# A chunked linear-attention and GELU kernel: end decays from transposed rows, state products inside the attention runs, more turns on the DMA crossbar, another order of loads, and every queue's order written out

## The chip, the cores and the metric

One Trainium2 chip; the program runs on one of its cores. The time is device microseconds of one execution. Five engines with a queue each work in parallel and wait for one another through semaphores: TensorE (PE; PEld is its weight load), VectorE (DVE), ScalarE (ACT), GpSimd (POOL) and SyncE (SP). Transfers are issued from the queues of SyncE, ScalarE and GpSimd and run on 16 DMA engines that all share.

## The reference

`q`, `k`, `v` and `alpha` are 4 x 8 heads x 768 tokens x 48, float32. A gated recurrence runs over the tokens of each head, and its output feeds a two-layer network with a tanh GELU:

```python
for t in range(S):
    state = alpha[:, :, t, :, None] * state + np.einsum('bhd,bhe->bhde', k[:, :, t], v[:, :, t])
    y[:, :, t] = np.einsum('bhd,bhde->bhe', q[:, :, t], state)
x = np.ascontiguousarray(y.transpose(0, 2, 1, 3)).reshape(B * S, H * D)      # 3072 x 384
h = x @ w_in                                                                 # 3072 x 2048
g = 0.5 * h * (1.0 + np.tanh(c * (h + 0.044715 * h * h * h)))
return g @ w_out                                                             # 3072 x 384
```

## The kernel before

The 768 tokens are cut into six chunks of 128. A pair is one chunk of two batch rows, so there are twelve pairs, 0 to 11; pair m is chunk m // 2. Inside a chunk the recurrence becomes products. With `cum` the running sum of ln(alpha) in the chunk, b = exp(cum) and binv = exp(-cum), one has q' = q b and k' = k binv; the masked product of q' and k' (`at`, then `atm`) times v gives what the chunk adds by itself, and q' times the carried state gives the rest. At the chunk's end the state is (state + k'^T v) times the end decay, exp of the sum over the whole chunk.

Steps of a pair, by the names that the written order uses (a number behind the dot tells steps of one kind in one pair apart):

- `load`: alpha, q, k, v, issued by GpSimd (line 308), each 128 tokens by 16 rows of 48. The loads are numbered in the order of LOADS: 12 is v of pair 0, 13 and 15 to 17 are the quarters of w_in, 18, 19, 24 and 29 the quarters of w_out, 20 to 23 are a, q, k, v of the first row of pair 2, 25 to 28 those of its second row, 30 to 33 a, q, k, v of pair 3, 34 to 37 of pair 4, 38 to 41 of pair 5, 42 to 45 of pair 6, 46 to 49 of pair 7, and so on to 65.
- `ln` (ScalarE, 361), `cum` (TensorE, 378): the sums, a product with a triangle of ones. For pairs 2 to 9 eight more products with a column of ones (380) give the chunk's whole sums with the head dimension on the partitions; `bend` (ScalarE, 401) takes their exp, `end` (VectorE, 516) spreads them. Pairs 0 and 1 are packed in another way and have products of their own (346, 350).
- `b`, `binv` (ScalarE, 407); `qp`, `kp` (VectorE, 418).
- the turn of q' and k' to head dimension on partitions: `t` (TensorE, 428) with eviction `ev` (446) for pairs 0 to 6, a crossbar transpose `turn` issued by SyncE (466) for pairs 7 to 11.
- `attn` (489), four `mask` (VectorE, 496), `y`: per row, products of q' with the state (543) and of `atm` with v (546) into one bank; `x` copies it (553).
- the turn of x: `tx` (560) with `xe` (564) for pairs 0 to 5, a crossbar `turn` for each row (472) for pairs 6 to 11.
- `kv` (506) and `st` (528, 531): the new state.

The network for pair m: `l1m.0` to `l1m.7` (line 572: 6 products of 256 columns each, for two of the 16 blocks of 128 hidden units), each with a `gelu` (578); `l2m.0` to `l2m.7` (591: 4 products of 384 columns, a quarter of the hidden units for one batch row's 128 tokens). The rows of pairs 0 and 1 share one second layer, l20.0 to l20.15, where l20.4 n to l20.4 n + 3 use quarter n of w_out. `ot` copies a result (603), `store` writes it (616).

All order is static. `tasks()` lists every step with its inputs, a cost for each engine that may do it, and the buffers that it takes; `Scheduler.order()` lays them out. Steps in FIRST (A ScalarE, V VectorE, P TensorE, S SyncE, G GpSimd) go on their engine's queue in just that order; after FIRST the planner picks the rest itself by its costs. Each engine then runs its queue in order. The planner knows the landing of a load from its own sum of transfer times, except where LANDED names the load:

```python
            if t.name in self.landed:
                t.done = self.landed[t.name]
```

LANDED holds loads 0 to 33 (among them "load.24": 30100, "load.25": 31000, "load.28": 32900, "load.29": 34800, "load.30": 36700, in ns). The written order of before ends within pair 3. PSUM is cut into `ca` (one of two banks), `yk` (two banks, for t, y, tx, kv) and `ff` (four, for the network's sums and some of `at`). DECAYS ties the ScalarE steps that need its ln/exp table to places between blocks of gelu, since it holds one table at a time.

Of the kernel before, what the change touches and what calls it, by code (L numbers as in the profile page):

```python
# [16 lines left out]
    cum=530, cum_packed=1500, t8=450, t4=225, attn=340, kv=170, inter=170, intra=205, tx=168, l1_4=655, l1_2=340, l2=655,  # L17
    qk2=910, qk1=500, ev8=650, ev4=350, mask=640, st=1090, st0=545, end=110, attn2=590, vb=320, vb_act=480, ring=1300, ring_issue=670, out=2050, lead=600, receipt=1400, receipt_hw=1000, xc=520, xe=330, ot=540,
    ev8_act=960, ev4_act=520, xc_act=450, xe_act=450, ot_act=450,
    strip=1700, cast=1900, weight=2080, dma=2100, issue=1100, wissue=760, sp=100, store=2600, turn=1250, landed=2200, xbar_qk=1500, xbar_x=1000, late_x=2500, late_qk=1200, piece=330, late_k=1500, piece_issue=450, begin=620, cast_0=1300, share=1200, cast_1=1900, ln_packed=1040, cold=380, fill=216, zero=1100,  # L20
# [26 lines left out]
class Scheduler:  # L47
# [16 lines left out]
    def order(self):  # L64
# [107 lines left out]
class _Kernel:  # L172

    BLOCKS = ((0,), (1,), (2,), (3,), (4,), (5,), (6,), (7,), (8,), (9,), (10,), (11,))
    DECAYS = {-1: (0, 1), 1: (2, 3), 2: (4,), 3: (5,), 4: (6, 7), 5: (8,), 6: (9,), 7: (10,), 8: (11,)}

    SPLIT = (2,)
    EARLY = (0, 1)
    LOADS = ('gatea 0 1', 'v0', 'gatek 0 1', 'in 0', 'v1', 'in 1', 'in 2', 'in 3', 'out 0', 'out 1', '2a', 'out 2', '2b', 'out 3', '3', '4', '5', '6', '7', '8', '9', '10', '11')
# [7 lines left out]
        A:table.0 A:load.2 A:load.3 S:load.0 S:load.1 S:load.4 A:ln0.0 S:load.5 P:fill.7 P:cum0.0 A:ln0.1 G:gate.0 G:load.12 S:load.6 P:cum0.1 A:b0.0 S:load.7  # L187
        A:bend0.0 V:qp0.0 A:binv0.0 A:binv0.1 S:load.8 V:kp0.0 P:fill.2 P:t0.0 A:b0.1 V:ev0.0 P:fill.1 P:t0.1 S:load.9 A:ev0.1 V:qp0.1 S:load.10 A:bend0.1
        P:fill.3 P:attn0.0 V:kp0.1 G:gate.1 S:load.11 P:t0.2 G:load.13 V:mask0.0 A:ev0.2 P:t0.3 G:load.14 V:mask0.1 A:ev0.3 P:fill.1 P:t0.4 V:ev0.4 P:fill.1
        P:attn0.1 A:ln1.0 G:load.15 P:t0.5 V:mask0.3 P:cum1.0 A:ev0.5 G:load.16 V:vb0.0 A:ln1.1 V:end0.0 P:y0.0 V:mask0.2 G:load.17 P:kv0.0 A:binv1.0 P:cum1.1  # L190
        V:st0.0 A:x0.0 G:load.18 A:vb0.1 V:kp1.0 P:tx0.0 A:b1.0 P:y0.1 V:xe0.0 G:load.19 V:qp1.0 P:t1.1 A:x0.1 A:bend1.0 G:load.20 A:b1.1 P:fill.1 P:t1.0
        A:ev1.0 V:ev1.1 G:load.21 V:qp1.1 P:fill.1 P:kv0.1 V:st0.1 G:load.22 A:binv1.1 P:tx0.1 P:attn1.0 V:xe0.1 G:load.23 P:t1.2 V:kp1.1 P:l10.0 A:ev1.2
        G:load.24 V:mask1.0 P:t1.3 A:bend1.1 P:t1.4 V:mask1.1 G:load.25 A:ev1.3 P:l10.1 V:ev1.4 G:load.26 A:vb1.0 P:t1.5 P:attn1.1 G:load.27 V:ev1.5 P:y1.0
        G:load.28 P:l10.3 V:end1.0 V:vb1.1 V:mask1.2 G:load.29 A:gelu0.0 P:kv1.0 P:l10.2 V:mask1.3 A:x1.0 G:load.30 P:l10.5 A:gelu0.1 V:st1.0 A:gelu0.3 P:y1.1
        G:load.31 P:l10.4 A:gelu0.5 V:x1.1 P:tx1.0 A:gelu0.2 P:tx1.1 P:l10.6 G:load.32 V:xe1.1 A:gelu0.4 V:xe1.0 P:l10.7 A:gelu0.6 G:load.33 P:l11.0 A:gelu0.7
        P:l11.6 A:gelu1.0 P:l11.5 A:gelu1.6 P:l11.7 A:gelu1.5 P:l11.2 A:gelu1.7 P:l11.4 A:gelu1.2 P:l11.3 A:gelu1.4 P:l11.1 A:gelu1.3 P:kv1.1 P:l20.0
        A:gelu1.1 P:l20.4 P:l20.1 A:ln2.0 P:l20.2 P:cum2.0 P:l20.5 A:b2.0 A:binv2.0 P:l20.9 A:bend2.0 V:kp2.0 A:ln2.1 P:l20.6 V:st1.1 P:cum2.1 V:qp2.0 P:l20.8
        A:b2.1 A:binv2.1 P:t2.0 P:l20.3 V:kp2.1 A:ev2.0 V:qp2.1 P:l20.10 A:bend2.1 P:attn2.0 P:t2.1 V:mask2.1 P:l20.7 A:ev2.1 V:mask2.0 P:l20.14 A:ln3.0
        P:attn2.1 P:y2.0 V:mask2.2 P:l20.13 V:mask2.3 P:l20.12 V:x2.0 P:cum3.0 A:ot0.0 V:ot0.1 P:y2.1 A:ot0.2 S:store0.0 S:store0.1 P:tx2.0 P:l20.11 A:x2.1
        S:store0.2 V:xe2.0 A:b3.0 P:tx2.1 P:l20.15 V:xe2.1 A:binv3.0 V:end2.0 P:l12.0 V:ot0.3 A:bend3.0 P:l12.1 V:qp3.0 S:store0.3 P:kv2.0 P:l12.2 V:st2.0  # L200
        A:gelu2.0 P:l12.3 V:end3.0 V:kp3.0 A:gelu2.1 P:l12.4 A:gelu2.2 P:t3.0 A:gelu2.3 P:t3.1 A:gelu2.4 V:ev3.0 P:l12.5
# [9 lines left out]
    TURN_QK, TURN_X = (7, 8, 9, 10, 11), (6, 7, 8, 9, 10, 11)  # L211
# [10 lines left out]
    BUFS = dict(ca=1, yk=2, ff=4, la=3, qp=4, kp=4, b8=2, kn=2, qkT=4, atm=6, x=3, ot=5, bend=3, ends=8,  # L222
                a=6, q=5, k=5, vb=6)

    def __init__(self, ctx, tc, q, k, v, alpha, w_in, w_out, out):
# [22 lines left out]
        self.ones = const.tile([C, 1], F16, name="ones")  # L248
# [314 lines left out]
    def turned_x(self, u, i, c, b):  # L563
        return lambda e: self.copy(e)(self.xT[c % self.NX][:, :, b, :], u["xT_ps", i])
# [356 lines left out]
```

## Time and profile before

| | |
|---|---|
| time, median of 3 runs | 177.35 us (176.74 to 177.91) |
| span of the profiled execution | 175.3 us |
| instructions | 4440 |
| hT products (line 572), 576 | 69.4 us busy, weight loads beside them 61.1 |
| acc products (line 591), 416 | 69.0 us busy |
| at products (line 489), 192, 64 x 128 by 128 | 8.0 us busy |
| intra products (546), 192, 48 columns | 8.7 us busy |
| state products (543), 80, 96 columns | 6.7 us busy |
| products with ones (380), 64, 1 column | 3.8 us busy |
| ScalarE table loads | 18 of 1283 ns |
| GpSimd's DMA queue | 17.70 MB, 60.8% of 16 engines' span |
| SyncE's and ScalarE's loads and crossbar | 10.49 MB, 24.8% |

The span runs from the program's first instruction to its last. Busy time of TensorE counts a product until its end, and products overlap: eight products of 183 ns that follow each other every 25 ns are done in 0.2 us. So what a product costs is read from the chain, in which a group's length is the time until the next group starts. A load has two times, that of its issue on a queue and that of its landing, and the DMA row of the slices shows how full the engines are in between.

### The profile page before, as it was taken

What the parts mean: (1) busy time and instruction counts of PE and PEld (TensorE: products, weight loads), DVE (VectorE), ACT (ScalarE), POOL (GpSimd) and SP (SyncE); (2) the same over time, 40 slices, a digit from 0 to 9 for tenths busy, and PEclk for the clock granted to TensorE, in tenths of its full rate; (3) what the DMA queues carried; (4) which work ended last, traced back from release to release, by engine and by line L of the source; (5) the groups of instructions that cost most, each with busy time, mean ns of one, the idle gap of its engine ahead of it and who ended that gap; (6) DMA issues with size and microseconds to landing.
All of it is one profiled execution on the core that took longest, in us unless ns stands there. A gap on an engine that the chain in (4) does not pass through costs nothing.

```text
span 175.3 us, 4440 instructions
## 1 busy us (share of the span) xinstructions
PE 170.4 (97%) x1845; PEld 135.4 (77%) x1845; DVE 96.8 (55%) x192; ACT 128.9 (74%) x213; POOL 57.7 (33%) x64
## 2 busy tenths in 40 slices
PE   7989999999999999999999999999999999999993
PEld 2667999667987896797798698698697697796973
DVE  6499920356888993795598897495426405000000
ACT  4677999666968668768788967977987984481941
POOL 2496348977645776576720000000000000000000
PEclk9999999999999999999999999999999999999999
DMA  4999999999999999999999992271271360401102
GB/s 138 307 262 224 210 243 238 246 205 207 249 273 204 242 256 220 217 226 199 200 264 224 200 136 80 54 172 52 47 187 28 90 165 4 115 20 49 45 0 90
DMA packets 49620, 28.86 MB, mean 165 GB/s; under 512 B 37696, under 2 KB 46016, under 8 KB 49600
## 3 DMA queue, kind: packets, MB, share of 16 engines
q0 software_dynamic: 26464, 17.70, 60.8%
q1 hardware_dynamic: 22592, 10.49, 24.8%
q10 hardware_dynamic: 544, 0.39, 0.8%
q8 instruction: 14, 0.23, 0.6%
q14 instruction: 6, 0.05, 0.1%
HBM read 25.17 MB, written 4.72 MB: 170 GB/s over the span
## 4 chain that ended last, share of the span: by engine, by line
PE 90%; DMA 6%; DVE 1%; issue 0%; ACT 0%; SPq 0%; POOL 0%
PE hT L572 36%; PE acc L591 36%; DMA v<-in_v_dram 4%; PE at L489 4%; PE qkT_ps L428 3%; PE yps L546 3%; PE kv L506 2%; PE yps L543 2%; DMA a<-in_alpha_dram 2%; PE cum L378 2%; PE xT_ps L560 1%; PE cum L380 1%; SPq L305 0%; ACT qkT L446 0%; DVE vb L389 0%
## 5 line engine op out<-in xcount | busy, mean ns | idle before, releaser
L572 PE MATMUL hT<-xT,w_in 128*128 128x256 bf16 x576 | 69.4, 273 | 0.0
L578 ACT ACTIVATE gT<-hT 128x512 bf16<-128x512 f32 x96 | 56.3, 600 | 17.7 <-PE hT L572 14.2
L591 PE MATMUL acc<-w_out,gT 128*128 128x384 bf16 (+3 forms) x416 | 69.0, 313 | 0.0
L572 PEld LDWEIGHTS <-w_in 128*128 128x128 bf16 x576 | 61.1, 114 | 1.6
L591 PEld LDWEIGHTS <-gT 128*128 128x128 bf16 x416 | 36.9, 98 | 19.2
L496 DVE TENSOR_TENSOR atm<-at,ut 128x512 bf16<-128x512 f32 x48 | 30.1, 681 | 12.7 <-PE at L489 12.6
L418 DVE TENSOR_TENSOR qp<-q,b 128x768 bf16<-128x768 f32 (+1 forms) x15 | 11.9, 794 | 14.0 <-ACT b L407 11.7
L418 DVE TENSOR_TENSOR kp<-k,binv 128x768 bf16<-128x768 f32 (+1 forms) x15 | 11.9, 791 | 10.6 <-ACT binv L407 10.6
L603 ACT COPY ot<-acc 128x384 f32<-128x384 f32 (+3 forms) x17 | 7.4, 439 | 13.0 <-PE acc L591 12.9
L308 POOL DMA_DIRECT2D k<-in_k_dram x11 | 12.2, 1107 | 6.6 <-DVE atm L496 3.0
L308 POOL DMA_DIRECT2D vb<-in_v_dram x11 | 12.1, 1102 | 6.7 <-PE hT L572 1.7
L308 POOL DMA_DIRECT2D q<-in_q_dram x11 | 12.2, 1109 | 6.1 <-DVE atm L496 1.3
L308 POOL DMA_DIRECT2D a<-in_alpha_dram x11 | 12.2, 1114 | 5.9 <-DMA w_in<-in_moe_w_in_dram 1.3
L407 ACT ACTIVATE b<-cum 128x768 bf16<-128x768 f32 (+1 forms) x15 | 10.3, 683 | 3.6 <-PE cum L380 2.3
L280 ACT ACT_TABLE_LOAD x9 | 11.5, 1283 | 0.9 <-PEq L905 0.7
L578 ACT ACT_TABLE_LOAD x9 | 11.5, 1283 | 0.2
L407 ACT ACTIVATE binv<-cum 128x768 bf16<-128x768 f32 (+1 forms) x15 | 10.2, 681 | 0.1
L528 DVE TENSOR_TENSOR stmp<-kv,st 128x384 f32<-128x384 f32 x16 | 8.8, 552 | 2.0 <-PE kv L506 2.0
L553 DVE CAST x<-yps 128x384 bf16<-128x384 f32 x12 | 6.7, 556 | 4.7 <-PE yps L546 4.7
L531 DVE TENSOR_TENSOR st<-stmp,ends 128x384 bf16<-128x384 f32 x16 | 8.9, 558 | 0.6
L446 ACT COPY qkT<-qkT_ps 128x512 bf16<-128x512 bf16 (+1 forms) x9 | 6.5, 728 | 3.7 <-PE qkT_ps L428 3.5
L546 PE MATMUL yps<-vb,atm 128*128 128x48 bf16 x192 | 8.7, 183 | 0.4 <-DVE vb L389 0.4
(65 smaller groups left out, 156.7 us busy)
## 6 DMA issues: line engine op xcount, KB each, us to landing
out_dram<-ot SPq DMA_DIRECT2D x19, 192.0 KB, 5.2
a<-in_alpha_dram POOLq DMA_DIRECT2D x9, 384.0 KB, 12.5
q<-in_q_dram POOLq DMA_DIRECT2D x9, 384.0 KB, 11.6
k<-in_k_dram POOLq DMA_DIRECT2D x9, 384.0 KB, 11.7
vb<-in_v_dram POOLq DMA_DIRECT2D x9, 192.0 KB, 11.6
w_in<-in_moe_w_in_dram POOLq DMA_DIRECT2D x4, 384.0 KB, 9.3
w_out<-in_moe_w_out_dram POOLq DMA_DIRECT2D x4, 384.0 KB, 11.1
out_dram<-ot SPq DMA_DIRECT2D x9, 96.0 KB, 1.8
```

Of the source, the lines that this page charges most:

```text
L280: nc.scalar.add_instruction(mybir.InstLoadActFuncSet(name=nc.get_next_instruction_name(), act_func_set_id=i, engine=mybir.EngineType.Activ ...
L308: dma(u[t][:, lo:hi].rearrange("t b h d -> t (b h) d"), src.rearrange("b h s d -> s (b h) d")[c * C:(c + 1) * C])
L407: self.nc.scalar.activation(u[n].rearrange("t i h d -> t i (h d)")[:, lo:hi], cum, AF.Exp, scale=1.0 if n == "b" else -1.0)
L418: self.nc.vector.tensor_tensor(out, rows, b, op=ALU.mult)
L496: self.nc.vector.tensor_tensor(u["atm", i][:, o], u["at", i][o], self.ut[:, None, :].to_broadcast([self.C, self.H // 2, self.C]), op=ALU.mult)
L528: nc.vector.tensor_tensor(s, acc, old, op=ALU.add)
L531: nc.vector.tensor_tensor(new.rearrange("f p (o d) -> f (p o) d", o=2), acc.rearrange("f p (o d) -> f (p o) d", o=2), ends, op=ALU.mult)
L546: nc.tensor.matmul(y[:, h, :], u["atm", i][:, h % 2, h // 2, :], u["vb"][:, i, h, :], start=c == 0, stop=True, skip_group_check=True)
L572: self.nc.tensor.matmul(h[:, s], w_in[:, j, nt % 4 + s], self.xT[c % self.NX][:, j, lo:hi].rearrange("p g t -> p (g t)"), start=j == 0, st ...
L578: return lambda e: self.nc.scalar.activation(self.gT[c % self.NG][:, nt:nt + 2, lo * self.C:hi * self.C], f.pop(("h", c, lo, nt)), AF.Gelu ...
L591: self.nc.tensor.matmul(f["acc", c, b][:, lo:hi], self.gT[c % self.NG][:, nt, b * self.C:(b + 1) * self.C], self.w_out[:, nt, lo:hi], star ...
L603: self.copy(e)(f["ot", c, b][:, sl], f["acc", c, b] if half is None else f["acc", c, b, half][:, sl])
```

## The change

- **End decays.** The products with ones and `bend` go for pairs 2 to 9. `b` becomes a float32 tile; its last 32 token rows are transposed on VectorE in four steps (`tr`), and `end` reads the last column.
- **State products.** For pairs 3 to 11 the products of q' with the state are issued at the end of `attn`, as 16 products of 64 rows by 48 columns, into two banks ordered by the parity of the head; `y` adds the intra products to them.
- **Crossbar.** q' and k' of pairs 5 and 6 and x of pair 5 move to it; x of both rows of a pair goes in one transpose; xT is stored row by row.
- **Loads.** Four gates on GpSimd hold the loads of pairs 7, 8, 9 and 10 until the turned q' of pairs 6, 7, 8 and 9 has landed. Loads from number 24 on are in another order.
- **Order.** FIRST reaches the end of the kernel. DECAYS and the column of ones are gone. LANDED is as it was. Buffers: b and binv 2 each, x 2 (now of both rows), bend 2, stmp 1.

```diff
-    cum=530, cum_packed=1500, t8=450, t4=225, attn=340, kv=170, inter=170, intra=205, tx=168, l1_4=655, l1_2=340, l2=655,
+    cum=330, cum_packed=1500, t8=450, t4=225, attn=340, kv=170, inter=170, intra=205, tx=168, l1_4=655, l1_2=340, l2=655,
...
-    LOADS = ('gatea 0 1', 'v0', 'gatek 0 1', 'in 0', 'v1', 'in 1', 'in 2', 'in 3', 'out 0', 'out 1', '2a', 'out 2', '2b', 'out 3', '3', '4', '5', '6', '7', '8', '9', '10', '11')
+    LOADS = ('gatea 0 1', 'v0', 'gatek 0 1', 'in 0', 'v1', 'in 1', 'in 2', 'in 3', 'out 0', 'out 1', '2a', 'out 2', '2b', 'out 3', '3', '4', '5', '6', 'gateT 6 0', '7', 'gateT 7 0', '8', 'gateT 8 0', '9', 'gateT 9 0', '10', '11')
...
     FIRST = """
...
+        P:attn1.0 V:xe0.1 G:load.23 G:load.37 G:load.34 G:load.27 G:load.36 P:t1.2 P:l10.0 V:kp1.1 V:mask1.0 V:mask1.1 P:t1.3 A:ev1.2 A:bend1.1 P:t1.4
+        A:ev1.3 P:l10.1 V:ev1.4 V:vb1.0 P:attn1.1 P:t1.5 V:mask1.2 G:load.25 P:y1.0 P:l10.3 P:l10.2 A:gelu0.0 A:gelu0.1 A:vb1.1 V:mask1.3 V:ev1.5
+        A:gelu0.3 P:l10.5 P:y1.1 V:x1.0 P:tx1.0 A:x1.1 G:load.26 G:load.24 G:load.29 P:l10.4 A:gelu0.2 A:gelu0.5 A:gelu0.4 G:load.41 G:load.30
+        G:load.33 G:load.28 P:tx1.1 V:end1.0 V:xe1.0 V:xe1.1 P:kv1.1 P:l10.7 P:l11.0 A:gelu0.7 P:l11.4 P:l11.6 A:gelu1.0 A:gelu1.6 A:gelu1.4 P:l11.3
+        P:l11.7 P:kv1.0 A:gelu1.7 A:gelu1.3 P:l10.6 P:l11.5 P:l11.2 A:gelu0.6 A:gelu1.5 A:gelu1.2 P:l11.1 A:gelu1.1 V:st1.0 V:st1.1 P:l20.0 P:l20.1
+        P:l20.2 P:l20.5 A:ln2.0 P:cum2.0 A:b2.0 A:binv2.0 P:l20.6 P:l20.3 P:l20.7 V:qp2.0 A:ln2.1 P:cum2.1 A:b2.1 V:kp2.0 P:t2.0 V:qp2.1 A:binv2.1
+        V:kp2.1 P:l20.10 G:load.42 G:load.31 P:l20.4 A:ev2.0 P:attn2.0 P:t2.1 P:l20.9 V:mask2.0 V:mask2.1 G:load.32 V:tr2.0 V:tr2.1 G:load.44 P:l20.14
+        A:ev2.1 P:attn2.1 V:mask2.2 V:mask2.3 V:tr2.2 V:tr2.3 V:end2.0 P:y2.0 P:l20.13 P:l20.8 A:ln3.0 P:cum3.0 P:y2.1 A:x2.0 A:ot0.2 P:tx2.0 V:x2.1
+        A:b3.0 P:l20.12 A:ot0.1 V:tr3.0 V:xe2.0 V:tr3.1 P:tx2.1 V:xe2.1 V:tr3.2 P:l20.11 P:l20.15 A:binv3.0 A:ot0.0 P:kv2.0 P:l12.0 P:l12.5 G:load.38
+        P:l12.2 P:kv2.1 V:qp3.0 V:st2.0 G:load.43 A:ot0.3 G:load.40 V:tr3.3 V:end3.0 V:kp3.0 P:l12.4 V:st2.1 A:gelu2.0 A:gelu2.2 A:gelu2.5 P:t3.0
+        A:ev3.0 P:l12.1 P:kv3.0 P:l12.6 P:kv3.1 P:l12.7 A:gelu2.1 V:st3.0 A:gelu2.4 G:load.35 A:gelu2.6 A:gelu2.7 P:t3.1 P:l12.3 V:st3.1 A:gelu2.3
+        P:l22.0 V:ev3.1 P:attn3.0 A:ln4.0 G:load.45 P:l22.1 P:l22.2 V:mask3.2 V:mask3.3 P:l22.3 P:cum4.0 V:mask3.0 V:mask3.1 P:y3.0 V:x3.0 P:l22.4
+        A:ln5.0 A:ot2.0 A:b4.0 V:tr4.0 V:qp4.0 P:y3.1 P:l22.5 A:x3.1 P:tx3.1 V:xe3.1 P:tx3.0 V:xe3.0 A:binv4.0 A:ln6.0 S:store0.3 S:store0.2 V:tr4.1
+        P:l22.6 P:l22.7 V:kp4.0 P:l13.0 P:l13.5 P:kv4.0 A:gelu3.0 A:ot2.1 P:l13.6 P:t4.0 P:l13.2 V:tr4.2 V:tr4.3 V:end4.0 V:st4.0 A:gelu3.6 A:gelu3.5
...
+        S:turn5.0 S:turn5.1 P:l23.3 V:qp6.0 V:end5.0 A:binv6.0 S:turn6.0 S:store2.0 V:tr6.1 P:l14.0 V:kp6.0 A:ot3.0 P:l14.2 P:kv5.1 A:gelu4.0
...
+        S:store10.0 S:store10.1 P:l111.2 P:l111.5 A:gelu11.0 A:gelu11.2 P:l111.1 A:gelu11.5 A:gelu11.1 P:l111.6 P:l111.4 P:l111.3 A:gelu11.6
+        A:gelu11.4 A:gelu11.3 P:l111.7 P:l211.0 P:l211.1 A:gelu11.7 P:l211.4 P:l211.5 P:l211.6 P:l211.7 A:ot11.1 P:l211.8 V:ot11.2 S:store11.2
+        P:l211.9 A:ot11.3 S:store11.3 S:store11.1 P:l211.2 P:l211.3 A:ot11.0 S:store11.0
-    TURN_QK, TURN_X = (7, 8, 9, 10, 11), (6, 7, 8, 9, 10, 11)
+    TURN_QK, TURN_X = (5, 6, 7, 8, 9, 10, 11), (5, 6, 7, 8, 9, 10, 11)
+    INTER = (3, 4, 5, 6, 7, 8, 9, 10, 11)
...
+    def turn_x_dma(self, u, c, b):
+        return lambda e: self.nc.sync.dma_start_transpose(
+            self.xT[c % self.NX][:, b:b + 2].rearrange("d u j t -> d (u j) t"), u["x"].rearrange("t u n -> t (u n)"))
...
+            if carried:
+                c, b = carried
+                y = [self.tile("yk", [C, 2, H // 2, self.D], F32, "yps") for _ in range(2)]
+                for i in units:
+                    st = self.state[b + i][c % 2]
+                    for p in range(H // 2):
+                        for o in range(2):
+                            sl = slice(64 * o, 64 * o + 64)
+                            nc.tensor.matmul(y[o][:, i, p, :], u["T"][sl, 0, i, p, :], st[sl, p, self.D * o:self.D * o + self.D],
+                                             start=(i, p) == (0, 0), stop=False, skip_group_check=True)
...
+    def last_row(self, u, o, half):
...
+            rows = u["rows"][96:128]
+            lo, f = o * D + 32 * half, 64 * o + 32 * half
+            self.nc.vector.transpose(u["tr"][f:f + 32, :, 0:32], rows[:, lo:lo + H * 2 * D].rearrange("t (g n) -> t g n", n=2 * D)[:, :, 0:32])
...
+    def y_heads(self, u, o):
...
+            for i in range(2):
+                for p in range(self.H // 2):
+                    self.nc.tensor.matmul(y[:, i, p, :], u["atm", i][:, o, p, :], u["vb"][:, i, 2 * p + o, :],
+                                          start=False, stop=True, skip_group_check=True)
...
+        return lambda e: self.nc.gpsimd.tensor_copy(self.gate[:, 0:1], u["T"][:, j, 0, 0, 0:1] if r == "T" else u[r][:, j, 0, 0:1])
...
-        s = self.s = Scheduler(self.BUFS, self.fill, 60000, self.FIRST, self.LANDED)
+        s = self.s = Scheduler(self.BUFS, self.fill, 0, self.FIRST, self.LANDED)
```

The last argument but two is the time until which the planner puts idle products into gaps of TensorE by itself; the written idle products at the start are the same in both.

## The prediction

> **What bounds the kernel now.** I read the page first (shares, slices, chain), then the chain in order of time, then GpSimd's issues, the crossbar transposes and the end.
>
> ```profile
> PE 170.4 (97%) x1845; PEld 135.4 (77%) x1845; DVE 96.8 (55%) x192; ACT 128.9 (74%) x213; POOL 57.7 (33%) x64
> PE 90%; DMA 6%; DVE 1%; issue 0%; ACT 0%; SPq 0%; POOL 0%
> ```
>
> TensorE is the bound. From 22 us to 172.7 us the chain (start, length, what) never leaves it, and pieces meet end to end, so a product removed there is time removed, and a wait put there is time added:
>
> ```profile
> 29.75 2.60 PE acc L591 x16
> 32.35 0.16 PE cum L378
> 32.52 0.08 PE cum L380 x4
> 32.60 1.97 PE acc L591 x12
> 34.57 0.16 PE cum L378
> ...
> 43.40 0.65 PE acc L591 x4
> 44.05 1.31 PE hT L572 x12
> ```
>
> ```profile
> 61.54 0.55 PE at L489 x16
> 62.10 0.28 PE kv L506 x4
> 62.37 1.97 PE hT L572 x18
> 64.34 0.17 PE yps L543 x4
> 64.51 0.20 PE yps L546 x8
> ...
> 73.12 0.89 PE qkT_ps L428 x16
> ```
>
> Under that chain the loads run at their own limit until 98.6 us: slices 2 to 23 of the DMA row stand at 9. GpSimd's queue in the stage that matters (start, length, what, and the idle time before it):
>
> ```profile
> 19.10 0.88 POOL L308 DMA_DIRECT2D vb<-in_v_dram  x1 [1.43 <-DMA w_in<-in_moe_w_in_dram]
> 21.01 0.56 POOL L325 DMA_DIRECT2D w_out<-in_moe_w_out_dram  x1 [1.03 <-DMA w_in<-in_moe_w_in_dram]
> 22.92 0.90 POOL L308 DMA_DIRECT2D a<-in_alpha_dram  x1 [1.35 <-DMA w_in<-in_moe_w_in_dram]
> ```
>
> By the trace's landing marks these three land at 29.1, 31.0 and 31.9 us, 9 to 10 us after their issue, and all loads of this queue land in the order of their issue. Each adds a fixed interval: 1.8 us for a pair's alpha, q or k, 1.4 for its v, 1.95 for a quarter of w_out, and 0.87, 0.66, 0.55, 0.46 for half of a pair's a, q, k, v. A load moved back by one pair's tile thus lands 1.8 us later, whoever waits.
>
> **What TensorE is spared.** The products with `ones` go: a pair's cumulative sums took 0.50 us with them (85.78 to 86.28) and 0.32 without (pair 10, 124.72 to 125.04), so 0.18 x 8 pairs = 1.4 us. The turns of q' and k' of pairs 5 and 6 go to the crossbar: 2 x 0.89 = 1.8 us; x of pair 5: 2 x 0.17 = 0.3 us. The state products of pairs 3 to 11 change from 8 of 128 rows by 96 columns (2 x 0.17 us a pair) to 16 of 64 rows by 48. No row shows that shape. The nearest are `at`, where two 64-row products start 3 to 4 ns apart and a couple advances like one 128-row product, and L546, whose eight 48-column products take 0.20 us. So eight couples cost 0.21 us; without overlap 16 x 25 ns = 0.40 us. I take 0.21, being nearest to `at`: 0.13 x 9 = 1.2 us gained, the other end a loss of 0.5 us. Together 4.7 us.
>
> **What is added, under cover.** 32 transposes of 32 partitions by 256 f32 on VectorE have no row. They lie between the 164 ns of L516 (16 elements) and the 954 ns of L418 (768); on that slope 0.42 us, 13 us in all. Off go 4 evictions of 0.69 us, 2 of 0.35 and five copies of `ot`. VectorE is busy 39 of the 50 us from 60 to 110 us, so TensorE's chain hides it; uncovered, four in front of a mask would cost 1.7 us a pair. `b` written as f32 costs nothing: qp already ran at 1.04 ns an element with its f32 q. ScalarE loses 9 `bend` (1.7 us) and gains five copies of `ot` (2.4 us), table loads stay 18. `attn` now holds both `yk` banks until x is copied; behind it on TensorE wait kv and tx, covered by the layer products written between.
>
> **What the new order of loads costs.** After load.23 (pair 2's first v, 29.1 us) GpSimd now issues 37, 34, 27, 36, 25, 26, 24, 29, 41, 30, 33, 28, 42, 31, 32, 44, 38, 43, 40, 35: v, alpha and k of pair 4 go ahead of pair 2's second half and of the third quarter of w_out. Adding the intervals: load.25 (alpha of pair 2's second half) lands at 35.5 instead of 31.9, load.24 (w_out, third quarter) at 38.1 instead of 31.0, load.29 at 40.1 (35.5), load.30 (alpha of pair 3) at 43.3 (37.4), load.28 (v of pair 2's second half) at 45.2 (33.6), load.32 (k of pair 3) at 50.6 (41.0), load.35 (q of pair 4) at 59.6, and 61.4 with the 1.75 us that four stores took between 42 and 58 us. The table of landings by which the order was laid out still gives loads 24 to 33 their old times.
>
> TensorE, in its new order, at the durations of the chain:
> - l20.0 at 29.6; seven quarters of 0.65 and cum2.0 bring it to 34.3. cum2.1 needs load.25 and a logarithm (35.5 + 0.53 + 0.15): waits to 36.2. Behind it stands everything, TensorE being in order.
> - cum and t2.0 to 36.8; l20.10 waits for load.24 to 38.1.
> - Six quarters, two attn, t2.1, y2.0: 43.6. cum3.0 needs load.30 and a logarithm of 0.84: 44.3. y2.1 needs load.28: 45.3. Then three quarters, y, two tx, a kv: l12.0 at 48.1, against 44.05 in the chain.
> - Four l12 and kv2.1: 50.9; t3.0 needs kp3.0 (50.6 + 0.95 + 0.15): 51.7. The rest of l12 and all of l22 with their attention work: 62.7.
> - l13.0 needs xe3.0, which stands on VectorE behind qp4.0, so behind load.35: 61.4 + 0.95 + 0.7 + 0.25 = 63.3.
>
> The same point in the chain is 58.5 us: 4.8 us late, savings up to there counted. Still to come of the 4.7 us: `ones` of pairs 5 to 9 0.9, state products of eight pairs 1.0, turns 2.1: 4.0 us.
>
> A row bears on these waits: the idle products at 1.2 to 4.4 us take 427 ns a piece, those at 6.8 us 215 ns, although the granted clock reads 1.00 in both; after the longest wait between them and the dense part (0.58 us at 12 us) nothing is slow. From 34.3 to 38.1 us TensorE would now do 0.6 us of work. The Trainium skill (TensorE: Matmul & The Clock Gate, Part 1) says that an idle window of about 3.4 us halves the clock until a busy window has passed; no wait of before is long enough to show it. By that rule some 3.4 us of products run at half pace, an estimate of 1.7 us lost, of which the waits at 44 and 45 us would swallow most.
>
> **The crossbar and the end.** turn5 and turn6.0 run while the gate holds the loads back, so at the quiet landing; attn5.0 comes 7 us after turn5.0 is issued, and needs 4.1 (1.3 for the issue before turn5.1, 2.8 to land).
>
> ```profile
> L472 SPq DMA_TRANSPOSE xT<-x x12: 1184/1206/1465, 93.1 to 149.3; - x12
> ...
> DMA to landing us min/median/max: 2.3/2.3/5.9
> ```
>
> The 5.9 is the one at 93.1 us, among loads; 2.3 holds after them. x of pair 5 turns after the gate has let pair 7 in: from y5.1 to l15.0 TensorE has 3.2 us of work, the copy takes 0.7 and the landing 2.6 (between 2.3 for 3 blocks and 2.8 for 8) to 5.9, so 0.1 to 3.4 us of wait. l18.0 has 6.1 us after cum9.0 for a turn that needs 5.9 if quiet. I take 0.6 us for both, bounds 0 and 5. At the end the last piece is now a copy of 384 columns with a 192 KB store, instead of 64 columns with 32 KB:
>
> ```profile
> 172.69 0.21 ACT L603 COPY ot<-acc 128x64 f32<-128x64 f32 x1 [0.20 <-PE acc L591]
> ```
>
> A 384-column copy takes 0.48 us, and late 192 KB stores land in 1.85 us against 1.49: +0.6 us.
>
> **Sum.** 4.8 - 4.0 + 0.6 + 0.6 = +2.0 us on a span of 175.3, so 177.3. The median lies 2.05 us over that span: 179.4 us.
>
> **The rivals.** (1) The loads don't hold TensorE: they land soon enough although reordered. Then 177.35 - 4.7 + 0.6 + 0.6 = 173.9 us. For it: a wait has to outlast each of six joints, and in the old order they had up to 2 us in hand. Against it: landing in order at fixed intervals, in every load of this queue. It decides at load.25 landing before 34 us. Chance 0.25. (2) The crossbar becomes the wait: one transpose for both x, SyncE's queue in order with turn9.2 behind turn10.0, loads let in by the gates. If each of pairs 5 to 9 waits 1 us more than I took, 184.4; for it the 5.9 us landing, against it the 2.3 once loads are out. Chance 0.13. (3) The clock gate of the skill in the starved stage: at its row's ratio of 2, up to 1.7 us more, 181.1. Chance 0.07. My forecast has 0.55, its own range 177.5 to 182 by the bounds above (state products +1.7, stores not in the way -1.7, crossbar up to +2).
>
> The range 174.0 to 183.5 leaves out half of (1) and half of (2). A change under 1% can't be told here (the three runs span 0.7%): faster than 175.6 has 0.25, slower than 179.1 has 0.52 (two thirds of the forecast, less a little, and both slow rivals), the rest 0.23.
>
> **What would show it.** Right: idle time in TensorE of 1 to 2 us ended by DMA or by ScalarE's logarithm near 34, 37 and 44 us; hT of the second block starting near 48 us; L380 gone; 16 state products in 0.21 us behind each `at`; after 65 us TensorE dense again. Wrong: no gap there, or hT of block 2 at 44 us; or gaps in front of hT from 90 us on, with releaser xT, which is rival 2.

## The result and the profile after

The kernel after the change takes 190.76 us (median of 4 runs, 190.41 to 191.59), beside 177.13 us for the kernel before in the same comparison: a ratio of 1.077, interval 1.0735 to 1.0808. It is slower, as forecast, but by 13.6 us and not by 2, and outside the range. The profiled execution has a span of 188.8 us (175.3 before). Some kernels below spread over several per cent from run to run; for these the fastest runs are named, and their ratios go by them.

The page of the changed kernel: busy time by engine, three rows of the 40 slices (4.72 us each), and the shares of the chain that ended last.

```profile
PE 168.7 (89%) x1813; PEld 131.1 (69%) x1815; DVE 107.6 (57%) x217; ACT 125.5 (67%) x206; POOL 58.6 (31%) x68
PEclk9999999969999999999999999999999999999999
DMA  4999999999999200477993997998999917312202
GB/s 140 311 265 197 214 224 203 217 197 200 219 261 275 57 0 3 93 169 181 145 309 71 229 167 99 233 115 188 232 187 157 241 46 155 108 42 63 87 0 83
...
DMA 42%; PE 31%; DVE 9%; ACT 5%; issue 5%; POOL 5%; SPq 1%; POOLq 0%
```

TensorE has slightly less work (168.7 us against 170.4) in a span that is 13.5 us longer, and the chain, which was TensorE's for 90%, is now 42% transfers. The DMA row says where. It stands at 0 in slices 15 and 16 (66 to 75 us), and then it is busy until about 150 us, where the loads of before were done at 98.6. The work was not taken away from the transfers; it was pushed back.

The early stretch first, TensorE in order of time (start, length, what, and the idle time before it with what ended it):

```profile
37.28 0.32 PE L415 MATMUL cum<-la,ut_h 128*128 128x384 f16 x1 [2.37 <-ACT la L398]
...
38.97 2.28 PE L666 MATMUL acc<-w_out,gT 128*128 128x384 bf16 x8 [0.92 <-DMA w_out<-in_moe_w_out_dram]
...
49.28 2.13 PE L647 MATMUL hT<-xT,w_in 128*128 128x256 bf16 x18
...
53.61 0.40 PE L462 MATMUL qkT_ps<-ident,kp 128*128 128x128 bf16 x4 [1.16 <-DVE kp L452]
...
64.47 1.47 PE L647 MATMUL hT<-xT,w_in 128*128 128x256 bf16 x12
```

These are the waits of the forecast, in their places: cum2.1 for the logarithm of load.25 (forecast to 36.2, here 37.3), l20.10 for load.24 (38.1, here 38.97), the network's second block at 49.3 (48.1), k' of pair 3 at 53.6 (51.7). The loads land within 1.2 us of the forecast: load.25 at 36.7 (35.5), load.24 at 38.9 (38.1), load.29 at 40.8 (40.1), load.28 at 46.4 (45.2), load.32 at 51.8 (50.6), load.35 at 60.4 (61.4). Load.23, the last one ahead of the new order, is itself 1.2 us late (30.35 for 29.1), so the intervals behind it are closer still. l13.0 starts at 64.47 us, against 63.3 forecast and 58.5 in the chain of before:

```profile
58.51 0.66 PE hT L572 x6
```

What was not forecast comes after that point. Waits of TensorE over 0.25 us from 64.5 us to the end add up to 11.0 us (none before the change). A wait is counted here from where the next product would usually have started; the idle times in the rows, which run from the modelled end of a product, are up to 0.16 us shorter. The six largest are 2.10 at 93.8 us (hT, for the turned x), 1.97 at 146.2 and 0.96 at 115.1 (attn, for turned q' and k'), 1.96 at 119.8 and 1.27 at 106.3 (cum, for a logarithm), 1.19 at 128.0 (turned x). Two of their rows:

```profile
95.90 0.81 PE L647 MATMUL hT<-xT,w_in 128*128 128x256 bf16 x6 [1.94 <-DMA xT<-x]
121.74 0.49 PE L415 MATMUL cum<-la,ut_h 128*128 128x384 f16 x2 [1.80 <-ACT la L398]
```

The chain in that stretch (start, length, what):

```profile
71.25 0.20 PE yps L533 x16
...
95.71 5.51 DMA qkT<-qp
101.22 0.02 issue
101.27 0.08 issue
101.35 0.02 POOL gate L351
101.37 0.60 issue
101.99 4.81 DMA a<-in_alpha_dram
106.80 0.02 issue
106.82 0.85 ACT la L398
107.67 0.04 issue
107.72 0.48 PE cum L415 x2
...
115.38 0.02 POOL gate L351
115.40 0.61 issue
116.03 4.79 DMA a<-in_alpha_dram
...
121.74 0.49 PE cum L415 x2
```

This is a loop. The turn of q' of one pair takes 5.5 us (five stores were issued on the same queue just ahead of it), the gate then lets go the alpha of the next pair, which needs 4.8 us to land on an empty queue, the logarithm 0.85, and cum of the next pair starts; from it come b, q' and the next turn. cum of pair 7 starts at 93.28, of pair 8 at 107.72, of pair 9 at 121.74: 14.4 and 14.0 us a round. TensorE's own work is some 12.1 us a pair (from start to start, 48 hT products of 109 ns, 32 acc products of 162 ns, and 1.7 us for the rest). So it has to wait some 2 us a round, in whichever place comes first; between these three cum it waited 3.4 and 2.9 us, with the rest of its work laid elsewhere. Two groups of the page, the gates and VectorE's transposes (busy time and mean ns, then the idle time before them):

```profile
L351 POOL CAST gate<-qkT 128x1 f32<-128x1 bf16 x4 | 1.0, 243 | 59.0 <-DMA qkT<-qp 59.0
L567 DVE STREAM_TRANSPOSE tr<-b 32x256 f32<-32x256 f32 x32 | 14.0, 438 | 2.1 <-ACT b L441 1.2
```

GpSimd, which only issues loads at this stage, stood 59 us at the four gates, 30.5 of them at the first. The empty stretch of the DMA row lies in that first wait: the loads ahead of the gate had landed by 63.7 us, and the gate let go at 83.7.

### The profile page after: what moved, and what is told of

Read it like the earlier page. It is cut to its first block, busy times and chain, and to the rows that moved or that the text cites. A ratio compares the mean times of both kernels' runs of the same rounds, so it can differ in the third digit from the quotient of the medians.

```text
span 188.8 us, 4392 instructions
## 1 busy us (share of the span) xinstructions
PE 168.7 (89%) x1813; PEld 131.1 (69%) x1815; DVE 107.6 (57%) x217; ACT 125.5 (67%) x206; POOL 58.6 (31%) x68
## 3 DMA queue, kind: packets, MB, share of 16 engines
q0 software_dynamic: 26464, 17.70, 57.8%
HBM read 25.17 MB, written 4.72 MB: 158 GB/s over the span
## 4 chain that ended last, share of the span: by engine, by line
DMA 42%; PE 31%; DVE 9%; ACT 5%; issue 5%; POOL 5%; SPq 1%; POOLq 0%
PE acc L666 14%; PE hT L647 13%; DMA q<-in_q_dram 11%; DMA a<-in_alpha_dram 9%; DMA qkT<-qp 8%; DMA w_out<-in_moe_w_out_dram 7%; DMA xT<-x 4%; DMA k<-in_k_dram 3%; DVE tr L567 3%; DVE qp L452 2%; DVE kp L452 2%; ACT la L398 2%; POOL w_in L358 2%; ACT L317 1%; PE at L524 1%
## 5 line engine op out<-in xcount | busy, mean ns | idle before, releaser
L647 PE MATMUL hT<-xT,w_in 128*128 128x256 bf16 x576 | 70.3, 273 | 3.4 <-DMA xT<-x 3.0
L666 PE MATMUL acc<-w_out,gT 128*128 128x384 bf16 (+3 forms) x416 | 69.7, 316 | 0.9 <-DMA w_out<-in_moe_w_out_dram 0.9
L653 ACT ACTIVATE gT<-hT 128x512 bf16<-128x512 f32 x96 | 53.3, 600 | 15.9 <-PE hT L647 14.4
L666 PEld LDWEIGHTS <-gT 128*128 128x128 bf16 x416 | 37.6, 98 | 21.2 <-issue 1.7
L351 POOL CAST gate<-qkT 128x1 f32<-128x1 bf16 x4 | 1.0, 243 | 59.0 <-DMA qkT<-qp 59.0
L678 ACT COPY ot<-acc 128x384 f32<-128x384 f32 (+2 forms) x22 | 10.2, 462 | 12.0 <-PE acc L666 10.6
L567 DVE STREAM_TRANSPOSE tr<-b 32x256 f32<-32x256 f32 x32 | 14.0, 438 | 2.1 <-ACT b L441 1.2
L398 ACT ACTIVATE la<-a 128x768 f16<-128x768 f32 (+1 forms) x11 | 8.6, 786 | 9.8 <-DMA a<-in_alpha_dram 9.8
L441 ACT ACTIVATE b<-cum 128x768 f32<-128x768 f32 (+1 forms) x15 | 10.3, 687 | 6.4 <-issue 3.2
## 6 DMA issues: line engine op xcount, KB each, us to landing
out_dram<-ot SPq DMA_DIRECT2D x19, 192.0 KB, 4.0
vb<-in_v_dram POOLq DMA_DIRECT2D x9, 192.0 KB, 9.9
```

What stands on the lines that cost most here:

```text
L398: self.nc.scalar.activation(u["la"][:, lo:hi, :, 0:self.D], u["a"][:, lo:hi], AF.Ln)
L441: self.nc.scalar.activation(u[n].rearrange("t i h d -> t i (h d)")[:, lo:hi], cum, AF.Exp, scale=1.0 if n == "b" else -1.0)
L567: self.nc.vector.transpose(u["tr"][f:f + 32, :, 0:32], rows[:, lo:lo + H * 2 * D].rearrange("t (g n) -> t g n", n=2 * D)[:, :, 0:32])
L647: self.nc.tensor.matmul(h[:, s].rearrange("p (g t) -> p g t", t=self.C), w_in[:, j, nt % 4 + s], self.xT[c % self.NX][:, lo:hi, j], start= ...
L653: return lambda e: self.nc.scalar.activation(self.gT[c % self.NG][:, nt:nt + 2, lo * self.C:hi * self.C], f.pop(("h", c, lo, nt)), AF.Gelu ...
L666: self.nc.tensor.matmul(f["acc", c, b][:, lo:hi], self.gT[c % self.NG][:, nt, b * self.C:(b + 1) * self.C], self.w_out[:, nt, lo:hi], star ...
```

## The experiments

The theory after the result had two parts: the order of loads costs what was forecast in the early stretch, and the rest comes from the crossbar and the gates together, by the loop above or by something else. Unless said otherwise an experiment starts from the changed kernel. All were compared with the kernel before on the same chip (177.0 to 177.3 us).

**Rising order of loads.** Loads 24 to 45 go in the order of their numbers in FIRST; the gates stay.

```diff
-        ... G:load.23 G:load.37 G:load.34 G:load.27 G:load.36 P:t1.2 ...
+        ... G:load.23 G:load.24 G:load.25 G:load.26 G:load.27 P:t1.2 ...
```

> The changed kernel, with loads 24 to 45 on GpSimd put back into rising order (2b, the last quarters of w_out, then pairs 3, 4, 5, 6); gates and everything else as changed. Theory (the order of loads starves TensorE up to 65 us, the gates later, each by itself): the waits at 34, 38 and 52 us go, hT of block 3 starts near 58 instead of 64.5 us, granted clock 1.00 throughout, and the gated stage begins 6 us earlier: 184 to 185.5 us. Rival (the gated stage sets the end by a clock of its own, the starved stage being covered): 189 to 191.

185.74 us, ratio 1.045 (1.038 to 1.052): 5.0 us come back, and hT of block 3 starts at 59.1 us. In its waits of TensorE (total, times, longest) the early ones are gone but for one of 0.8 us for k' of pair 3. What is left are the late ones:

```profile
PE hT L644 <- DMA xT<-x: 3.3, 2, 2.3
PE cum L412 <- ACT la L395: 2.5, 2, 1.8
PE at L521 <- DMA qkT<-qp: 1.8, 1, 1.8
```

So the first term of the sum is right, and 8.7 us are still missing. One thing of the theory did not hold: the granted clock was not 1.00 throughout, but 0.50 from 91.1 to 94.6 us, from the end of the wait of 2.3 us for turned x on.

**No gates.** The changed kernel without its four gates on turned q'.

```diff
-    ..., '6', 'gateT 6 0', '7', 'gateT 7 0', '8', 'gateT 8 0', '9', 'gateT 9 0', '10', '11')
+    ..., '6', '7', '8', '9', '10', '11')
```

> The changed kernel without the four gates on GpSimd; order of loads as changed. Theory (a loop cum of a pair, b, q', its turn, gate, alpha of the next pair, ln, cum of that pair takes 14 us where TensorE's work for a pair is 12.3): the waits at cum of pairs 7 to 10 and at attn of pair 10 go, waits for turns among loads of 1 to 2 us at l15 and l16 stay: 182 to 185 us. Rival (the turns suffer more among open loads than behind gates): 189 us or more, with hT and at waiting for turns of 5 to 6 us in every pair to 100 us.

201.6 and 202.7 us in the two fastest of four runs (206.9 and 208.8 in the others), ratio 1.137 (1.125 to 1.149). The loop is gone and some 11 us are lost. The theory fell; the rival had the direction, but neither saw waits of this size. SyncE's queue (start, length of the issue, what) and the waits of TensorE:

```profile
79.67 2.79 SPq L497 DMA_TRANSPOSE qkT<-kp  x1
82.57 12.62 SPq L497 DMA_TRANSPOSE qkT<-qp  x1
95.28 0.59 SPq L688 DMA_DIRECT2D out_dram<-ot  x1
95.97 5.87 SPq L497 DMA_TRANSPOSE qkT<-kp  x1
```

```profile
PE at L521 <- DMA qkT<-kp: 15.6, 3, 12.4
```

An issue that takes 1.2 us on quiet queues holds SyncE for 12.6 us here, and the turns land 10 to 23 us after their issue, against 2.8. The loads suffer with them: none lands between 83.7 and 97.3 us, where one landed every 1.8 us before. They do not stand still, for their queue still moves 118 GB/s in this stretch (203 from 70 to 80 us), and from 97.3 us on six land 1.1 to 1.4 us apart. The trace's packets point to the reason. From 88 to 90 us GpSimd's queue moved 150 packets with a mean of 1868 bytes and SyncE's 146 packets of 256 bytes, and from 100 to 102 us it was 199 and 201: one for one, which fits a transpose whose small packets each wait for a load's large one. The Trainium skill (DMA: Bandwidth & Descriptors, Queues, rings and completion order) says that each DMA engine goes round the queues it has work for, one packet at a time; the counts agree.

The same trace shows the clock. Each row is a stretch in us, its length, the busy us of TensorE, weight load, VectorE, ScalarE and GpSimd with their instructions, TensorE's granted clock, the view's DMA share (it can exceed 1), and GB/s:

```profile
88.00:90.00 2.00, 0.00 (x0) 0.00 (x0) 0.00 (x0) 0.00 (x0) 0.00 (x0) 1.00 1.37 159
90.00:92.00 2.00, 0.00 (x0) 0.00 (x0) 0.00 (x0) 0.00 (x0) 0.00 (x0) 0.68 1.36 171
...
100.00:102.00 2.00, 2.00 (x26) 1.10 (x21) 2.00 (x4) 0.00 (x0) 0.00 (x0) 0.50 1.52 110
102.00:104.00 2.00, 2.00 (x8) 0.99 (x7) 0.21 (x1) 0.00 (x0) 0.00 (x0) 0.50 1.65 114
```

Four us into the wait the clock falls to half, and it stays there until 104.4 us, though TensorE works again from 99.1. So a long wait is paid for twice.

**Both undone.** Rising loads and no gates: only the early waits and the loop are taken away.

> Both: loads in rising order and no gates; arithmetic, crossbar and the order on the other engines as changed. Theory: the two gains add up, 175 to 179 us, beside 177 of the kernel before. Rival (the rest of the change, crossbar turns and written order, costs time by itself): over 181.

206.2 and 209.2 us in the two fastest of four runs, ratio 1.169 (1.153 to 1.184); in the profiled run (209.6) waits of 16.6 us and 10.6 us in front of attn of pairs 5 and 6. My theory, a gain, fell. With no early waits the first turn of pair 5 goes out at 71.3 us, with 16 loads still to land (77.0 us and 14 in the run before this one).

**Alpha ahead of the gates.** The alpha loads of pairs 8 to 11 are issued ahead of the gate that held them back (they still stand behind the one before it), which cuts the loop between gate and logarithm.

```diff
-            loads[key] = s.add("load", {"POOL": cost}, n, emit, gate, land=...)
+            loads[key] = s.add("load", {"POOL": cost}, n, emit, [] if key[0] == "a" and key[1] > 7 else gate, land=...)
```

> The changed kernel with alpha of pairs 8, 9, 10 and 11 issued just ahead of the gate that held it back; gates and other loads as changed. Theory: the loop loses the load of alpha, so the waits at cum of pairs 8 and 9 (1.3 and 2.0 us) go and the wait moves to q', whose load is still behind the gate; 186 to 188.5 us. Rival (the loop does not set the pace, the turns do): 190 to 191, with the waits merely turned into waits for xT and qkT.

191.4 us, ratio 1.074 (1.063 to 1.085): no gain, as the rival had it. The late waits for the logarithm are gone; waits of 3.5 and 3.4 us for turned x, at 93.5 and 127 us, stand in their place. The loop isn't the only limit: the turns of x wait on SyncE's queue and among transfers as well. The waits after 64.5 us add up to 8.6 us here, 2.4 less than in the changed kernel; but each of the two long ones is followed by 3.4 us of granted clock 0.50 (97.1 to 100.6 and 131.3 to 134.7 us), where the changed kernel's clock stays at 1.00 after 42.9 us. So part of what the cut spares goes to the clock.

**Gates one pair later.** Rising loads; each gate holds the loads of one pair further on.

```diff
-    ..., '6', 'gateT 6 0', '7', 'gateT 7 0', '8', 'gateT 8 0', '9', 'gateT 9 0', '10', '11')
+    ..., '6', '7', 'gateT 6 0', '8', 'gateT 7 0', '9', 'gateT 8 0', '10', 'gateT 9 0', '11')
```

> The kernel with loads in rising order, and each gate one pair later: pair 7 is loaded with no gate, the turn of pair 6 lets pair 8 in, 7 lets 9, 8 lets 10, 9 lets 11. Theory (the loop cum, b, q', turn, gate, alpha, ln, cum is too long for one pair's 12.3 us of TensorE work; spread over two pairs it has room): no waits for alpha at cum of pairs 7 to 10 and none at attn of pair 10, only turns landing among loads left: 179.5 to 182 us, beside 185.7 with rising loads alone. Rival (the turns' landings, not the loop, hold TensorE): 184.5 or more, the waits merely standing in front of hT and at.

182.49 us, ratio 1.032 (1.027 to 1.036), 3.3 us better than rising loads alone and half a us above the theory's figure. The waits for the logarithm and for q' of pair 10 are gone, as the loop would have it; two waits of 2.4 us for turned x (88.6 and 120.0 us) and one of 1.0 for k' stay. This is the nearest that a kernel with the turns of pairs 5 and 6 on the crossbar came to the one before.

**Crossbar as before, inside the changed kernel.** Rising loads, the turns of pairs 5 and 6 back on TensorE, and one gate, at the turned k' of pair 7, before the loads of pairs 10 and 11.

```diff
-    TURN_QK, TURN_X = (5, 6, 7, 8, 9, 10, 11), (5, 6, 7, 8, 9, 10, 11)
+    TURN_QK, TURN_X = (7, 8, 9, 10, 11), (6, 7, 8, 9, 10, 11)
-    ..., '6', 'gateT 6 0', '7', 'gateT 7 0', '8', 'gateT 8 0', '9', 'gateT 9 0', '10', '11')
+    ..., '6', '7', '8', '9', 'gateT 7 1', '10', '11')
```

> Loads in rising order; q', k' of pairs 5 and 6 and x of pair 5 turned on TensorE again, as in the kernel before; no gate but one, at k' of pair 7, in front of the loads of pairs 10 and 11. All else as changed (end decays by VectorE, state products in the attention runs, one transpose for both x, written order). Theory (the turns of pairs 5 and 6 stand in the middle of the loads, and the gates that part the two are what costs; the rest of the change is worth 1.4 + 1.2 us less 0.6 at the end): 174 to 176.5 us. Rival (the written order or the new work on VectorE costs by itself): over 178.

191.24 us, ratio 1.080 (1.076 to 1.084). The theory missed by 15 us, and one wait has most of it:

```profile
PE at L521 <- DMA qkT<-kp: 8.7, 1, 8.7
```

The gate let eight loads go at once, and the turns of pair 8, issued at 105.9 and 108.1 us among them, landed after 11.2 and 11.8 us. From 114.4 to 124.6 us the granted clock then reads 0.50. The gate moved the collision on by one pair.

**The end as before.** The same, with the four small last pieces of the result back at the very end.

```diff
-        ... P:l211.4 P:l211.5 P:l211.6 P:l211.7 A:ot11.1 ... S:store11.1 P:l211.2 P:l211.3 A:ot11.0 S:store11.0
+        ... P:l211.2 P:l211.3 A:ot11.0 S:store11.0 P:l211.4 P:l211.5 P:l211.6 P:l211.7 A:ot11.1 ... S:store11.1
```

> As the run before it, and the last products in the old order: the small pieces of the last row come last. Theory: 0.6 us less than that run, the last copy 64 columns and 0.21 us, the last store landing in 1.5 us. Rival (the end is covered by other stores): the same within 0.2 us.

190.71 us (190.49 to 190.74), beside 191.24 (190.55 to 191.93) above. The medians differ by 0.53 us, but the traces don't put that at the end. From the start of the last 64 products to the end of the span it takes 9.01 us here and 8.95 above; the run profiled above lost more at another place, 1.40 us in front of hT at 62.7 us against 0.25. The term itself shows in the first two traces, where the chain's last group of products starts 7.98 us ahead of the end before the change (span 175.35) and 8.64 after it (188.76):

```profile
167.37 5.29 PE acc L591 x64
180.12 5.29 PE acc L666 x64
```

**The crossbar alone.** The kernel before, with the one line that moves the turns of pairs 5 and 6 and x of pair 5.

```diff
-    TURN_QK, TURN_X = (7, 8, 9, 10, 11), (6, 7, 8, 9, 10, 11)
+    TURN_QK, TURN_X = (5, 6, 7, 8, 9, 10, 11), (5, 6, 7, 8, 9, 10, 11)
```

> The kernel before with one part alone: q', k' of pairs 5 and 6 and x of pair 5 on the crossbar; no gates, the rest planned as before. Theory (a turn among running loads takes its turn packet by packet with them and lands after 10 to 20 us; no gate, so no loop): 190 to 205 us with one or two waits of some 10 us for qkT in front of at. Rival (2.1 us of TensorE work saved, landings of 5 to 6 us covered): 174.5 to 176.5.

198.2 us in the fastest of four runs, 202.9 to 205.4 in the others: one line costs 21 us or more. The waits of TensorE in its profiled run, the slowest:

```profile
PE at L489 <- DMA qkT<-kp: 17.9, 4, 9.1
PE hT L572 <- DMA xT<-x: 5.9, 1, 5.9
```

So this is the part of the change that has the price; the gates hold it down (190.8 us with them, 202 without) and add their own.

**End decays, state products and the joint turn of x, alone.** The kernel before with these parts only; crossbar and loads as before, the rest laid out by the same planner with the changed kernel's costs.

```diff
+    INTER = (3, 4, 5, 6, 7, 8, 9, 10, 11)
...
-        self.ones = const.tile([C, 1], F16, name="ones")
...
+                be = [s.add("tr", {"DVE": W["tr"]}, P + 25, self.last_row(u, o, half), ...) for o in range(2) for half in range(2)]
```

> The kernel before with two parts alone: end decays of pairs 2 to 9 by transposes on VectorE, and the state products of pairs 3 to 11 in the attention runs (with them x of both rows in one transpose). Crossbar from pair 7 (x from 6), loads, gates and the order to pair 3 as before, the rest planned by the same greedy rule. Theory (these two spare TensorE 1.4 and 1.2 us, VectorE and the banks have room): 174.4 to 175.5 us, L380 gone, 16 state products in 0.21 us, TensorE dense. Rival (four more steps of 0.44 us a pair on VectorE or the two held banks stand in front of mask and xT; or TensorE, earlier by 2 us, meets its first turns among more loads): 177 to 181 with waits for DVE or for xT.

180.03 us, ratio 1.016 (1.013 to 1.018). The 2.6 us spared don't appear; the rival had it, with its waits for VectorE. Seven waits over 0.25 us add up to 3.1 us, nearly all for VectorE (0.56, 0.36 and 0.68 us in front of kv, for the evictions of the next pair's q' and k', which queue right behind four transposes, at the 0.36 behind two), and the planner put eight idle products into a gap that it foresaw at 57.8 us, 1.75 us at 216 ns.

**End decays alone.** The same with `INTER = ()`.

> As the run before it, state products as in the kernel before: the end decays alone (and one transpose for both x). Theory: 1.4 us gained, 175.5 to 176 us, and so 1.2 us slower than with the state products. Rival (VectorE's 14 us more cost TensorE waits): 177.5 or more.

192.0 to 194.4 us in the four fastest of six runs, ratio 1.089 (1.083 to 1.095), where I expected a gain. The waits of TensorE in the profiled run, the slowest (196.4):

```profile
PE at L490 <- DMA qkT<-kp: 8.0, 2, 7.0
PE hT L613 <- DMA xT<-x: 2.0, 1, 2.0
```

The turns of pair 7 go out at 91.7 and 93.9 us, the first with five loads still to land (the last at 103.5), and need 12.1 and 12.4 us. In the kernel before, the first turn goes out at 93.1 us with four to land, a small one of x, and lands after 5.9; q' of pair 7 follows at 95.1 and needs 4.8, and the last load lands at 98.6. So a kernel in which q' of pair 7 goes out 3.4 us sooner brings its turns into the queue of loads. That the time spared on TensorE alone does this is not shown, since the planner laid out the rest anew: with the state products as well, q' of pair 7 goes out at 92.65 us with five loads to land, needs 8.4 us, and no wait in front of attn follows.

**No idle products.** The three parts alone, without the eight idle products.

```diff
-        s = self.s = Scheduler(self.BUFS, self.fill, 60000, self.FIRST, self.LANDED)
+        s = self.s = Scheduler(self.BUFS, self.fill, 50000, self.FIRST, self.LANDED)
```

> e10_two_parts with one edit: the eight idle products that its order puts on TensorE at 57.8 and 58.9 us go (1.75 us at 216 ns a piece); every other instruction and its order stay. Rounds decide: e10_two_parts had 180.03 us. Theory (idle products are time on the path, as 1.8 us of the chain): 178.3 us, 177.9 to 178.7. Rival (the turn of pair 7, issued at 92.65 us there with three loads still to land and 8.4 us to land itself, is then issued near 91 us and shares the queues with more loads, as in e11_decays_alone, issue 91.7, landing 103.8): a wait of 4 to 8 us in front of attn of pair 7, 183 to 190 us. A third outcome, 180 us, would say that the start of pair 7 hangs on the loads whatever TensorE does before it.

180.12 us (179.91 to 182.13): no change, the third outcome, though not for the reason given there. (In the kernel with the idle products five loads, not three, were still to land at 92.65 us.) The gap is VectorE's. In its trace (this profiled execution lies 2 us later from the start on) TensorE's queue at that place reads:

```profile
60.69 0.51 PE L601 MATMUL xT_ps<-ident,x 128*128 128x128 bf16 x6 [0.65 <-DVE x L592]
62.27 1.50 PE L613 MATMUL hT<-xT,w_in 128*128 128x256 bf16 x12 [1.07 <-DVE xT L605]
```

x and xT are both on VectorE's queue, around four masks and a q', and the idle products had only covered that wait. So the sum closes: 2.6 us spared, 3.1 us of waits shown and 2.05 us (0.81 + 1.24, beyond the usual step from product to product) covered by idle products leave +2.55, and TensorE's last group starts at 169.77 us against 167.21.

**Turns only after the last load.** The same with the crossbar from pair 8 on (x from pair 7), one pair later than before.

```diff
-    TURN_QK, TURN_X = (7, 8, 9, 10, 11), (6, 7, 8, 9, 10, 11)
+    TURN_QK, TURN_X = (8, 9, 10, 11), (7, 8, 9, 10, 11)
```

> e12_no_fill with the crossbar starting one pair later: q' and k' of pair 7 and x of pair 6 turn on TensorE, so that no turn is issued before the last load has landed (98.6 us). Adds 0.89 + 0.34 us of TensorE work and four evictions. Theory (a turn is only costly beside queued loads): every turn lands within 2.7 to 4 us, no wait over 0.8 us in front of attn, 179.0 to 180.0 us, whichever way e12_no_fill goes. Rival (the price lies with the crossbar's own issues or with VectorE): waits in front of attn or hT stay, over 181 us.

183.22 us, ratio 1.031 (1.027 to 1.036), above the theory's 179 to 180 and over the rival's 181, one of whose waits, in front of hT, is there. The theory's mechanism held all the same: the last load lands at 98.2 us, the first turn goes out at 103.6, every turn in the trace lands within 2.7 to 2.9 us but one of 4.6 beside a store, and nothing waits over 0.25 us in front of attn. The rest is 1.2 us of turns back on TensorE, one wait of 1.58 us at 118.6 us for x, whose copy came so late that even the quiet landing was too long, and a clock at half speed from 60.1 to 63.5 us. None of these versions is faster than the kernel before.

## Why the prediction was right in direction and wrong in size

- **What the new order of loads costs: right.** 4.8 us forecast, 6.0 us measured at l13.0 (64.47 against 58.5), and 5.0 us come back when the order is undone. Adding fixed intervals in the order of issue gave each landing to 1.2 us, and each wait in its place. The term was 1.2 us short, and 0.4 of that was there before the first of these waits, when l20.0 started (29.96 us for 29.6).
- **The clock gate: rival 3 happened, in part.** The granted clock in the windows of the changed kernel, by the columns above:

```profile
38.00:40.00 2.00, 1.08 (x6) 0.58 (x5) 1.03 (x2) 1.42 (x3) 2.00 (x3) 0.86 1.82 188
40.00:42.00 2.00, 2.00 (x15) 0.93 (x14) 0.16 (x1) 0.00 (x0) 1.61 (x2) 0.50 1.86 212
42.00:44.00 2.00, 2.00 (x16) 1.30 (x13) 1.96 (x4) 1.01 (x1) 1.42 (x2) 0.78 2.05 174
```

  Shares of 0.86, 0.50 and 0.78 mean half speed from about 39.4 to 42.9 us, 3.4 us. The eight acc products at 38.97 take 2.2 us where the chain of before has 1.3. The Trainium skill (TensorE: Matmul & The Clock Gate, Part 1) has the clock halved by an idle window of about 3.4 us until a busy one has passed; the length agrees, but the window need not be idle throughout: two waits of 2.4 and 0.9 us with 0.8 us of work between them were enough. Part of it is in the 1.2 us by which the first term was short. The granted clock of 1.00 that the prediction read at the idle products of 1.2 to 4.4 us was no measurement: the trace of before has no clock record ahead of 6.35 us, and the view counts such time as full speed.
- **What TensorE is spared: the work right, the time not.** The sixteen state products take 0.20 us, as the 0.21 of the forecast had it. But the kernel with only these parts is 2.8 us slower than before, not 2.6 faster.
- **What is added, under cover: right in the price, wrong about the cover.** The transposes take 438 ns for 420 forecast. "TensorE's chain hides it" was read from VectorE's share of a stretch. A share says nothing of four transposes in front of one eviction: in the three-part kernel transposes stand right ahead of the awaited copy in four of the seven waits, 2.2 of the 3.1 us.
- **The crossbar and the end: the step that failed.** 0.6 us taken, bounds 0 and 5; the waits after 64.5 us are 11.0 us. Each landing was priced by itself, by the 2.3 us and the 5.9 us of a row of before. That 5.9 is a turn of three blocks with the last four loads of the kernel still to land; it was no upper bound for a turn of eight among a full queue, which needs 10 to 23 us without gates. With them a turn of eight took up to 5.5 us, beside stores alone. And "turn5 and turn6.0 run while the gate holds the loads back, so at the quiet landing" is true of these two; what the gate does to the next pair's alpha wasn't followed. The round can be added up: cum 0.3, b 0.8, q' 1.0, the turn, gate and issue 0.8, a load on an empty queue 4.8 (from this trace; in the one before, a pair's load never meets an empty queue), the logarithm 0.85. That is 11.4 us with a quiet turn of 2.8 and 14.1 with one of 5.5, beside the 14.4 and 14.0 measured and the 12.1 us of a pair's work: hardly any slack for a turn that meets anything, be it only stores.
- **The end: right.** 0.6 us forecast; 0.66 measured, by the two chains shown above (8.64 against 7.98 us).
- **The sum, re-made:** 6.0 early, 11.0 late, 4.0 still to come as forecast, 0.6 at the end: 6.0 + 11.0 - 4.0 + 0.6 = 13.6, against 13.5 us of span. The 4.0 is the forecast's own figure and was not measured by itself; that the sum closes speaks for it. Rival 2, the crossbar as the wait, named the place and the mechanism at 1 us a pair for five pairs; it was about 2.

What stays open: whether end decays and state products could gain with VectorE's work in another order, and what the written order to the end of the kernel is worth, which no run tried by itself. No run took the turns of pairs 5 and 6 off the crossbar and left all turns quiet with the rest as changed either, so the share of the crossbar in the 13.6 us is read from the chain and from the experiments around it. Of the 202 us without gates the clock alone is an estimate of 2.6 us, half of the 5.3 us in which TensorE worked at half speed.

## What to carry to other kernels

A transfer of small packets that starts beside a queue of large ones is priced by what is still queued when it starts, not by the landings seen at the end of that queue; find the last load's landing first, and treat any step that brings the transfer ahead of it as a risk, even one that only spares the busy engine some time. A gate that orders transfers closes a loop through the compute engines: add up one round of it and hold it against the work of one round. And cover on an in-order engine is read from what stands in front of the one instruction that others wait for, not from the engine's busy share.

## What the runs showed of the hardware that was not expected

- Crossbar transposes and loads of 192-byte runs share the DMA engines packet by packet, 146 against 150 in 2 us, and both slow down: in the run without gates a turn of eight blocks goes from 2.8 to between 10 and 23 us, the queue of loads from 203 to 118 GB/s, with no load landing for 13.6 us.
- In these traces the granted clock is decided every 3.41 us, by how full the 3.41 us before were. In each of the 14 traces the changes of the clock lie on a grid of that step (to 1 ns), so a stretch at half speed lasts 3.4 us or a whole multiple of it: 13.7 in the run without gates (90.7 to 104.4 us), 17.1 with both undone. Call a window filled by the time that its products need at 0.42 ns a column (162 ns for 384 columns). Of the 707 windows at full speed 23 are followed by half speed, and these are filled to 36% at most; the other 684 are filled to 39% or more. Full speed comes back behind a window filled to 77% or more, with products at half speed counted double; 57% was not enough. So a wait of 8 us or more is caught 2.5 to 4.1 us after the last product, and of short waits it counts how much of them falls into one window. With the turns after the last load, waits of 0.81 and 1.23 us lie in the window from 56.7 to 60.1 us, which is filled to 36%, the highest of the 23; half speed follows (columns as above):

```profile
58.00:60.00 2.00, 0.84 (x9) 0.68 (x10) 1.91 (x5) 1.98 (x3) 1.31 (x3) 1.00 1.36 285
60.00:62.00 2.00, 2.00 (x13) 1.47 (x12) 1.93 (x5) 0.68 (x2) 1.41 (x2) 0.52 1.31 264
62.00:64.00 2.00, 2.00 (x22) 2.00 (x21) 1.25 (x3) 0.60 (x1) 1.53 (x2) 0.63 1.64 243
```

  The kernel without idle products has the same two waits (0.81 and 1.24 us), but there a border of the grid lies between them, at 61.3 us. The two windows are filled to 65% and 68%, and the clock stays at full speed.
